# Top-k attention with two MLPs: decoding the first two 64-bit weights with one VectorE operation per two pieces

## The chip, the cores and the metric

One Trainium2 chip, one core of it. The metric is device time in microseconds (us) of one execution of the whole program. A core has five engines with instruction queues of their own, which run in order and wait for each other through semaphores: TensorE (PE in the profile), VectorE (DVE), ScalarE (ACT), GpSimd (POOL) and SyncE (SP), which here only issues transfers for the 16 DMA engines.

## What is computed

```python
def reference(q, k, v, moe_w_in, moe_w_out, moe2_w_in, moe2_w_out):
    scores = q @ k.T / sqrt(64)              # 4 batches, 8 heads, 576 x 576, head size 64
    keep the 32 largest of each row, softmax over them
    x = attn @ v                             # as 2304 tokens x 512
    h = x @ moe_w_in;  g = h * sigmoid(h);   x = g @ moe_w_out      # 512 -> 2048 -> 512
    h = x @ moe2_w_in; g = elu(h);           x = g @ moe2_w_out
    return x
```

q, k and v are float32. The four weights (512x2048 or 2048x512) arrive as float64: a weight is scaled by a 64-bit scalar when it is drawn. One weight is 8.4 MB.

## The kernel before

**Tiles and slots.** The 2304 tokens make 18 chunks of 128 rows, and with 8 heads 144 tiles. The program is one sequence of slots, `slot(s)`, from -4 on; the order of every engine's queue is written out there by hand. Slot s holds the scores of tile s+1 (TensorE, `emit_qk`), the first half of the top-k of tile s and the second half of that of tile s-1 (VectorE: four MAX8 and three MATCH_REPLACE8, then the mask, line 590), the exponential (ScalarE, line 582), the split of the exponentials into two float16 halves (ScalarE line 610, GpSimd line 616), their transpose by DMA (line 619) and the product with V of tile s-3 (`emit_av`). From slot 12 (`LAG`) on it also holds a step of the first MLP, from slot 24 on one of the second (`emit_in`, line 695, and `emit_out`, line 743). Slots 0 to 11 hold no MLP step.

**Weights.** Each weight is 16 pieces of 128x512 numbers, 512 KB in float64. `w_load` (line 240) brings a piece as 1024 32-bit words to a staging place; `w_rest` (259) replaces the low word of each number by its top bits as an integer, on ScalarE (line 263) or GpSimd (265); `w_dec_ops` (267) makes the float32 bit pattern of the high word by two VectorE operations, masking and shifting the lower 27 bits into a PSUM tile y (278), then putting sign and top exponent bit to it (281); GpSimd adds the remainder (284). `PIECES` (807) says how many pieces are decoded in slots -2, -1, 0 and so on: 3, 3, then 5 per slot, 3 in slot 11. Slots -2 to 1 decode weight 0, slots 2 to 5 weight 1, slots 5 to 8 weight 2, slots 8 to 11 weight 3. `dv` (965) places them: after each top-k operation up to `per` decode operations are issued. Ten pieces of weight 3 are staged and decoded in halves of 256 columns, in buffers of the MLP that are still unused (`rows`, line 212).

**Scales and splits.** When a weight is decoded, `w_gram` (291) sums its squares on TensorE, `w_trace` (301) reduces that on VectorE, and `w_ops` (306) makes a power of two as its scale. Then each piece is split into two float16 halves. At a point of a slot (`w_point`, 919: p = 0, 1 or 2) TensorE forms the low halves of two pieces (`w_lo`, 320, lines 322 and 323), ScalarE writes them (`w_put`, line 327) and makes the high halves of two later pieces (`w_hi`, line 316, one operation of 1024 elements). `free` (896) lists the points that may be used; slots 3 to 11 use 3, 3, 2, 0, 3, 3, 1, 3, 3 of them.

**Loads.** All transfers are issued by SP in the order of the slots: at a slot's start loads of Q, K and V, the transpose `et` of the exponentials, then the weight loads of `wload` (line 983); at its end transposes of Q and K (`q_tp`, `k_tp`, lines 515 and 411) and the weight loads of `wnow`. The pieces of weight 0 are issued from slot -4 on: 2, 4, 2, 3, 5 in slots -4 to 0; later ones a slot before their decode, as far as the staging place is free (`freed`, 218). The first K transposes belong to slot -2.

Of the kernel before, what the change touches and what calls it, by code (L numbers as in the profile page):

```python
# [32 lines left out]
def kernel(  # L33
# [172 lines left out]

    sW = {}
# [7 lines left out]
        [16, 18, 20, 22, 24, 26, 28, 30, 14, 12, 16, 18, 20, 22, 24, 26],  # L215
        ["tt", "gg", "ux", 30, 28, 26, 24, "tt", "gg", "ux", 30, 28, "tt", "gg", (WEND - 1, "6"), "ux"],
# [4 lines left out]
        [(1, n) for n in range(8)] + [(1, 15), (1, 14)] + [(2, n) for n in range(6)],  # L221
        [(1, 15)] * 3 + [(2, 7), (2, 6), (2, 15), (2, 14)] + [(3, n) for n in range(5)] + [(3, 7), (3, 8), (3, 10), (3, 9)],
# [35 lines left out]

    def w_rest(j, n, e=None):
        low = raws[j, n, e].rearrange("p (x two) -> p x two", two=2)[:, :, 0]  # L260
        top = raws[j, n, e].bitcast(U16).rearrange("p (x four) -> p x four", four=4)[:, :, 1]
        if slot_now[0] < ON_ACT or n % 2 == 0:
            nc.scalar.activation(out=low, in_=top, func=AF.Copy, scale=2.0 ** -13)
        else:
            nc.gpsimd.tensor_scalar(low, top, 2.0 ** -13, 0.0, op0=ALU.mult, op1=ALU.add)

    def w_dec_ops(j, n, e=None):
        f = w_raw(j, n, Wi)
        if e is not None:
            f = f[:, e * 256:(e + 1) * 256]  # L270
        def word(x):
            return raws[j, n, e].rearrange("p (x two) -> p x two", two=2)[:, :, x]

        y = []

        def first():
            y.append(ps_h.tile([128, 512], F32, tag="h0", name="y").bitcast(I32)[:, 0:f.shape[1]])
            nc.vector.tensor_scalar(y[0], word(1), 0x07FFFFFF, 3, op0=ALU.bitwise_and, op1=ALU.logical_shift_left)  # L278
# [669 lines left out]
    def slot(s):  # L948
# [170 lines left out]
```

## Time and profile before

| | |
|---|---|
| three runs | 1118.25, 1122.69, 1123.08 us; median 1122.69 us |
| profiled execution | 1125.6 us; its span from first to last instruction 1123.8 us |
| busy in the span | TensorE 997.1 us (89%), VectorE 954.2 (85%), ScalarE 877.8 (78%), GpSimd 816.2 (73%) |
| DMA | 141.34 MB moved |
| VectorE, two decode operations, slots 0 to 4 | 25 and 25 instructions, 34.2 us busy |

The page of the profile gives busy times of each engine, the span in 40 slices, the chain of work that ended last and groups of instructions by source line. The span is cut further below into windows that are the kernel's slots. A share over the whole span mixes the lead-in, in which the weights are decoded, with the long stretch of MLP steps; the views by window keep them apart.

### The profile page before, as it was taken

What the parts mean: (1) busy time and instruction counts of PE and PEld (TensorE: products, weight loads), DVE (VectorE), ACT (ScalarE), POOL (GpSimd) and SP (SyncE); (2) the same over time, 40 slices, a digit from 0 to 9 for tenths busy, and PEclk for the clock granted to TensorE, in tenths of its full rate; (3) what the DMA queues carried; (4) which work ended last, traced back from release to release, by engine and by line L of the source; (5) the groups of instructions that cost most, each with busy time, mean ns of one, the idle gap of its engine ahead of it and who ended that gap; (6) DMA issues with size and microseconds to landing.
All of it is one profiled execution on the core that took longest, in us unless ns stands there. A gap on an engine that the chain in (4) does not pass through costs nothing.

```text
span 1123.8 us, 30899 instructions
## 1 busy us (share of the span) xinstructions
PE 997.1 (89%) x11956; PEld 716.2 (64%) x11956; DVE 954.2 (85%) x2215; ACT 877.8 (78%) x1541; POOL 816.2 (73%) x1001
## 2 busy tenths in 40 slices
PE   0266679589989999999998999999999999999997
PEld 0223336367766777777766777777677777777755
DVE  5999998999887999999997999999899999994000
ACT  5577768989877898989887898988777777776554
POOL 5779886887767777777776777878767777776643
PEclk9978989889999999999999999999999999999999
DMA  9999883565577655566586757467864544433100
GB/s 307 302 256 259 255 206 84 92 98 115 111 136 127 120 102 113 117 115 132 108 149 133 138 103 126 103 119 135 135 115 87 100 82 82 82 68 58 29 20 10
DMA packets 385746, 141.34 MB, mean 126 GB/s; under 512 B 361536, under 2 KB 368704, under 8 KB 385600
## 3 DMA queue, kind: packets, MB, share of 16 engines
q1 hardware_dynamic: 385600, 139.38, 59.6%
q8 instruction: 93, 1.52, 0.6%
q14 instruction: 53, 0.43, 0.1%
HBM read 52.17 MB, written 21.10 MB: 65 GB/s over the span
## 4 chain that ended last, share of the span: by engine, by line
PE 39%; POOL 20%; issue 12%; DVE 11%; DMA 7%; ACT 6%; SPq 1%; POOLq 0%; ACTq 0%; DVEq 0%
PE h L695 17%; PE a L743 15%; POOL t L723 5%; POOL gh L162 4%; DVE m L567 3%; POOL e L616 3%; DVE r L571 3%; DMA xt<-x 3%; PE S L532 3%; PE av L635 2%; DVE y L278 2%; DMA et<-e 2%; POOL W L616 2%; POOL x L162 1%; DVE e L590 1%
## 5 line engine op out<-in xcount | busy, mean ns | idle before, releaser
L695 PE MATMUL h<-xt,W 128*128 128x128 f16 x6912 | 412.0, 220 | 8.6 <-DMA xt<-x 8.6
L695 PEld LDWEIGHTS <-W 128*128 128x128 f16 x6912 | 396.5, 98 | 22.1 <-DMA xt<-x 8.9
L743 PE MATMUL a<-W,gh 128*128 128x512 f16 x1728 | 399.0, 380 | 3.9 <-POOL gh L162 2.0
L567 DVE MAX8 m<-r 128x8 f32<-128x576 f32 x432 | 312.8, 749 | 2.6
L743 PEld LDWEIGHTS <-gh 128*128 128x128 f16 x1728 | 159.6, 98 | 178.8 <-POOL gh L162 4.8
L162 POOL TENSOR_TENSOR gh<-t,gh 128x512 f16<-128x512 f32 x144 | 167.3, 1162 | 73.7 <-ACT gh L727 73.7
L571 DVE MATCH_REPLACE8 r<-m,r 128x576 f32<-128x576 f32 x288 | 213.8, 742 | 0.0
L723 POOL TENSOR_TENSOR t<-u,t 128x512 f32<-128x512 f32 x144 | 183.4, 1273 | 29.8 <-ACT u L717 23.4
L582 ACT ACTIVATE e<-S,bias,c 128x576 f32<-128x576 f32 x144 | 119.8, 832 | 52.0 <-DVE r L571 36.4
L727 ACT ACTIVATE gh<-t 128x512 f16<-128x512 f32 x144 | 90.2, 627 | 88.5 <-POOL t L723 87.6
L616 POOL TENSOR_TENSOR e<-e,e 128x512 f16<-128x512 f32 x87 | 100.9, 1160 | 78.5 <-ACT e L610 74.2
L567 DVE MAX8 m<-S 128x8 f32<-128x576 f32 x144 | 109.6, 761 | 36.0 <-PE S L532 35.6
L532 PE MATMUL S<-kt,qt 128*128 128x288 f16 (+1 forms) x640 | 99.0, 295 | 36.1 <-DVE sv L134 18.7
L532 PEld LDWEIGHTS <-qt 128*128 128x128 f16 (+1 forms) x640 | 56.7, 102 | 110.2 <-issue 41.2
L590 DVE SCALAR_TENSOR_TENSOR e<-S,m,e 128x576 f32<-128x576 f32 x144 | 115.3, 801 | 0.1
L571 DVE MATCH_REPLACE8 r<-m,S 128x576 f32<-128x576 f32 x144 | 107.6, 747 | 0.0
L616 POOL TENSOR_TENSOR W<-e,W 128x512 f16<-128x512 f32 x57 | 66.2, 1161 | 44.0 <-ACT W L610 38.8
L635 PE MATMUL av<-vt,et 128*128 128x64 f16 (+1 forms) x2100 | 79.3, 194 | 12.9 <-DMA et<-e 12.9
L635 PEld LDWEIGHTS <-et 128*128 128x128 f16 (+1 forms) x2240 | 73.1, 101 | 21.3 <-DMA et<-e 14.8
L610 ACT ACTIVATE e<-e 128x576 f16<-128x576 f32 x87 | 58.9, 677 | 27.8 <-DVE e L590 15.1
L322 PE MATMUL lo<-W,eye 128*128 128x512 f32 x84 | 56.9, 766 | 20.1 <-ACT W L327 19.0
L284 POOL TENSOR_TENSOR W<-W 128x512 int32<-128x512 int32 (+1 forms) x55 | 68.9, 1282 | 7.5 <-DVE W L281 2.5
(126 smaller groups left out, 1265.3 us busy)
## 6 DMA issues: line engine op xcount, KB each, us to landing
W<-in_moe_w_in_dram SPq DMA_DIRECT2D x32, 512.0 KB, 7.1
W<-in_moe_w_out_dram SPq DMA_DIRECT2D x22, 512.0 KB, 5.1
qd<-q SPq DMA_DIRECT2D x34, 256.0 KB, 4.5
kn<-in_k_dram SPq DMA_DIRECT2D x16, 288.0 KB, 3.3
qn<-in_q_dram SPq DMA_DIRECT2D x16, 256.0 KB, 3.5
out_dram<-o SPq DMA_DIRECT2D x16, 256.0 KB, 2.4
vd<-v SPq DMA_DIRECT2D x12, 320.0 KB, 2.4
vt<-vd SPq DMA_DIRECT2D x22, 160.0 KB, 2.8
```

The lines of the kernel that those rows point to most:

```text
L162: nc.gpsimd.tensor_tensor(dst, x, hi, op=ALU.subtract)
L532: nc.tensor.matmul(out=ps[n * e:n * e + n, a, 0:HALF], lhsT=qt[:, 2 * (t % 2) + p, n * e:n * e + n], rhs=kT[bh][:, a * HALF:(a + 1) * HALF ...
L567: nc.vector.max(st["m8"][:, i, :], src if i == 0 else st["r"])
L571: nc.vector.match_replace(out=fold(r) if i == 0 else r, in_to_replace=st["m8"][:, i, :], in_values=src if i == 0 else r, imm_value=LOW,)
L582: nc.scalar.activation(out=fold(e), in_=src, func=AF.Exp, scale=c[:, 0:1], bias=bias)
L590: nc.vector.scalar_tensor_tensor(e, src, st["m8"][:, n - 1, 7:8], e, op0=ALU.is_ge, op1=ALU.mult, accum_out=sums[ch][:, j:j + 1])
L616: nc.gpsimd.tensor_tensor(h[:, S + LO:2 * S], e[:, 0:SF], h[:, 0:SF], op=ALU.subtract)
L635: nc.tensor.matmul(out=avs[ch][n * e:n * e + n, bh[1], :], lhsT=et[:, c, n * e:n * e + n], rhs=vT[bh][:, x, y:y + D], start=(i == 0), stop ...
L695: nc.tensor.matmul(out=ps[:, f:f + 128], lhsT=w, rhs=xt[:, z, :], start=(kk == 0 and x == 0), stop=(kk == KDM - 1 and x == 2),)
L723: nc.gpsimd.tensor_tensor(t, u, t, op=ALU.add if l else ALU.mult)
L727: nc.scalar.activation(out=gh[:, 0, :], in_=gf[l, ch, i], func=AF.Copy)
L743: nc.tensor.matmul(out=acc, lhsT=gh[:, z, u * 128:(u + 1) * 128], rhs=W[:, n, w * 512:(w + 1) * 512], start=(m == 0 and x == 0), stop=(m = ...
```

## The change

Weights 0 and 1 (`SIGNED`) get another decode, in pairs of pieces (1024 numbers). The high word is only shifted left by 3, in one VectorE operation for the pair; its second operand is a zero, one element in PSUM that is broadcast (`zero_at`). The shift loses the sign. ScalarE therefore writes the sign of each number as a bfloat16 plus or minus one into the upper half of the low word, after the remainder, and the addition on GpSimd adds sign, exponent offset and remainder together. The result is half the number, which `shift` of `w_ops` makes good. Remainders and additions of weights 0 to 2 and of the whole pieces of weight 3 are done in pairs; the two VectorE operations of those are as before, but the addition follows the last of them.

The work is laid out anew: `PIECES` is 2, 2, 6, 6, 4, 6, 6, 4, 6, 4, 5, 5, 5, 3, so weight 1 ends in slot 4. The loads of weight 0 are 3, 2, 0, 3, 8 in slots -4 to 0; weights 1 and 2 load 4, 6, 6, 4, 6, 4 in slots 1 to 6. Weight 3 has 12 pieces in halves, in another order of staging places, and more of its loads at the end of the slot ahead. The points (`POINTS`, with a fourth at a slot's end) are 1, 2, 1, 3, 4, 3, 1, 4, 2 in slots 3 to 11. In slot 0 decode operations follow only a top-k operation, and small operations left at a slot's end go ahead of left decode operations.

```diff
+    SIGNED = (0, 1)
+    PAIR = 2
...
-        [16, 18, 20, 22, 24, 26, 28, 30, 14, 12, 16, 18, 20, 22, 24, 26],
-        ["tt", "gg", "ux", 30, 28, 26, 24, "tt", "gg", "ux", 30, 28, "tt", "gg", (WEND - 1, "6"), "ux"],
+        [16, 18, 20, 22, 24, 26, 28, 30, 12, 14, 16, 18, 20, 22, 24, 26],
+        ["tt", "gg", 28, 30, "ux", "tt", "gg", "ux", "tt", "gg", 28, 30, "ux", "tt", (WEND - 1, "6"), "gg"],
...
+            if n % 2 == 0:
+                raws[j, n, e] = Wi[:, r:r + 2 * PAIR, :].rearrange("p a x -> p (a x)")
...
     def w_rest(j, n, e=None):
-        low = raws[j, n, e].rearrange("p (x two) -> p x two", two=2)[:, :, 0]
-        top = raws[j, n, e].bitcast(U16).rearrange("p (x four) -> p x four", four=4)[:, :, 1]
-        if slot_now[0] < ON_ACT or n % 2 == 0:
+        low = w_word(j, n, e, 0)
+        top = w_half(j, n, e, 1, U16)
+        if e is None and slot_now[0] < ON_ACT or e is None and n % 4 == 0 or e == 0:
             nc.scalar.activation(out=low, in_=top, func=AF.Copy, scale=2.0 ** -13)
         else:
             nc.gpsimd.tensor_scalar(low, top, 2.0 ** -13, 0.0, op0=ALU.mult, op1=ALU.add)
+        if j in SIGNED:
+            nc.scalar.activation(out=w_half(j, n, e, 1, BF16), in_=w_word(j, n, e, 1).bitcast(F32), func=AF.Sign)
 
     def w_dec_ops(j, n, e=None):
...
+        def rest():
             nc.vector.scalar_tensor_tensor(
-                f, word(1), -(1 << 30), y[0], op0=ALU.bitwise_and, op1=ALU.bitwise_or
+                f, w_word(j, n, e, 1), 3, zero_at().bitcast(I32).to_broadcast([128, m]),
+                op0=ALU.logical_shift_left, op1=ALU.bitwise_or
             )
-            nc.gpsimd.tensor_tensor(f, f, word(0), op=ALU.add)
-
-        return [first, second]
+            add()
+
+        def add():
+            nc.gpsimd.tensor_tensor(f, f, w_word(j, n, e, 0), op=ALU.add)
+
+        def halves(x):
...
+        if j in SIGNED:
+            return [rest]
+        return [o for x in range(0, m, 512) for o in halves(x)]
+
+    zero0 = ps_v.tile([128, H, D], F32, tag="av", name="zero")[:, 0, 0:1]
+    zero = {}
+
+    def zero_at():
+        s = slot_now[0]
+        if s < 3:
+            return zero0
+        if s not in zero:
+            zero[s] = Sps[s][:, 0, HALF + 64:HALF + 65]
+            nc.vector.memset(zero[s], 0.0)
+        return zero[s]
...
-        return pow2_ops(m, *sW[j])
+        return pow2_ops(m, *sW[j], 1 if j in SIGNED else 0)
...
-    PIECES = (3, 3, 5, 5, 5, 5, 5, 5, 5, 5, 5, 5, 5, 3)
+    PIECES = (2, 2, 6, 6, 4, 6, 6, 4, 6, 4, 5, 5, 5, 3)
     ON_ACT = 3
+    POINTS = {3: (2,), 4: (1, 2), 5: (2,), 7: (0, 1, 2, 3), 9: (2,), 10: (0, 1, 2, 3), 11: (0, 1, 2, 3)}
...
-            decs[s].append((j, *x))
+            if x[1] is not None or x[0] % 2 == 0:
+                decs[s].append((j, *x))
...
-    free = [(s, p) for s in range(ends[0] + 1, LAG + 1) for p in range(3) if p == 2 or s not in held]
+    free = [(s, p) for s in range(3, LAG) for p in POINTS.get(s, (0, 1, 2)) if p > 1 or s not in held]
...
-        wload[(-5, -5, -4, -4, -4, -4, -3, -3, -2, -2, -2, -1, -1, -1, -1, -1)[n]].append((0, n, None))
+        wload[(-5, -5, -5, -4, -4, -2, -2, -2, -1, -1, -1, -1, -1, -1, -1, -1)[n]].append((0, n, None))
...
                 if o:
                     o.pop(0)()
+                elif s == 0:
+                    continue
...
-        while small_ops or dec:
-            dv([])
+        while small_ops:
+            small_ops.pop(0)()
+            if s < 0 and dec:
+                dec.pop(0)()
+        while dec:
+            dec.pop(0)()
...
+        w_point(s, 3)()
...
+        nc.vector.memset(zero0, 0.0)
```

The function `halves` holds the two operations of before, unchanged, for each half of a pair.

## Rows read from the trace of the kernel before

**Rows 1.** Busy tenths of the span in 40 slices, from the page.

```profile
PE   0266679589989999999998999999999999999997
...
DVE  5999998999887999999997999999899999994000
```

**Rows 2.** Busy time in a window (length, engines, PEclk, DMA share, GB/s), body.

```profile
800.00:1000.00 200.00, 200.00 (x2598) 149.44 (x2597) 189.24 (x424) 155.40 (x274) 140.97 (x181) 1.00 0.51 92
```

**Rows 3.** The same view of slots 0 to 4 and slot 6.

```profile
20.57:31.09 10.52, 1.38 (x7) 0.60 (x5) 9.61 (x17) 8.16 (x17) 6.93 (x7) 1.00 1.00 368
31.09:43.92 12.83, 1.04 (x6) 0.72 (x7) 12.62 (x29) 4.09 (x7) 8.94 (x9) 1.00 1.13 333
43.92:56.78 12.86, 6.07 (x72) 5.43 (x70) 12.62 (x28) 8.73 (x19) 10.29 (x12) 0.86 0.85 259
56.78:69.61 12.83, 8.67 (x29) 3.65 (x28) 12.62 (x30) 6.50 (x10) 10.54 (x13) 0.63 1.05 276
69.61:82.12 12.51, 8.48 (x33) 3.54 (x32) 12.30 (x27) 12.18 (x24) 8.53 (x11) 0.84 0.96 245
...
95.59:109.51 13.92, 5.63 (x86) 4.89 (x84) 12.99 (x32) 7.83 (x16) 12.43 (x14) 0.81 1.03 279
```

**Rows 4.** Groups by line and shape, slots 0 to 4 (busy us, mean ns).

```profile
L284 POOL TENSOR_TENSOR W<-W 128x512 int32<-128x512 int32 x24 | 30.4, 1293 | 4.6 <-DVE W L281 2.3 <-issue 0.9 <-DMA vn<-in_v_dram 0.8
L281 DVE SCALAR_TENSOR_TENSOR W<-W,y 128x512 int32<-128x512 int32 x25 | 17.2, 687 | 0.9
L278 DVE TENSOR_SCALAR y<-W 128x512 int32<-128x512 int32 x25 | 17.0, 681 | 0.7 <-DMA W<-in_moe_w_in_dram 0.6
...
L316 ACT ACTIVATE W<-W,sw 128x1024 f16<-128x1024 f32 x5 | 5.7, 1150 | 0.3 <-DVE sw L134 0.3
...
L327 ACT ACTIVATE W<-lo 128x512 f16<-128x512 f32 x8 | 4.4, 589 | 0.2 <-PE lo L323 0.2
...
L263 ACT ACTIVATE W<-W 128x512 int32<-128x512 uint16 x20 | 12.0, 659 | 2.2 <-DMA W<-in_moe_w_in_dram 2.2
```

**Rows 5.** VectorE in order of time in slot 1 (start, length).

```profile
33.89 0.68 DVE L278 TENSOR_SCALAR y<-W 128x512 int32<-128x512 int32 x1
34.60 0.69 DVE L281 SCALAR_TENSOR_TENSOR W<-W,y 128x512 int32<-128x512 int32 x1
35.20 0.08 DVE L571 MATCH_VALUE_LOAD r<-m,r 128x8 f32 x1
```

**Rows 6.** Groups by shape at other sizes, in the lead-in.

```profile
L281 DVE SCALAR_TENSOR_TENSOR W<-gh,y 128x256 int32<-128x256 int32 x6 | 2.5, 421 | 0.3
...
L263 ACT ACTIVATE t<-t 128x256 int32<-128x256 uint16 x4 | 1.5, 429 | 0.0
...
L284 POOL TENSOR_TENSOR W<-W,t 128x256 int32<-128x256 int32 x6 | 4.3, 740 | 0.2 <-DVE p L131 0.2
...
L162 POOL TENSOR_TENSOR q<-qn,q 128x1024 f16<-128x1024 f32 x1 | 2.1, 2142 | 0.4 <-ACT q L484 0.4
```

**Rows 7.** Waits from 20 to 82 us (total us, times, longest).

```profile
ACT W L263 <- DMA W<-in_moe_w_in_dram: 2.2, 3, 1.2
```

**Rows 8.** Busy time in stretches of 2 us at the start.

```profile
10.00:12.00 2.00, 0.00 (x0) 0.00 (x0) 1.90 (x4) 1.25 (x3) 2.00 (x2) 1.00 1.02 411
...
16.00:18.00 2.00, 0.10 (x1) 0.00 (x0) 1.86 (x6) 1.54 (x3) 0.23 (x1) 1.00 1.45 93
```

**Rows 9.** The start in order of time, SP and VectorE.

```profile
12.99 3.72 SPq L411 DMA_TRANSPOSE kt<-k  x2
...
21.90 0.76 DVE L567 MAX8 m<-S 128x8 f32<-128x576 f32 x1
```

**Rows 10.** TensorE and VectorE in order of time, slots 12 and 13.

```profile
176.26 1.02 PE L322 MATMUL lo<-W,eye 128*128 128x512 f32 x2
...
189.32 0.16 DVE L131 TENSOR_SCALAR p<-gram 128x1 int32<-128x1 int32 x1 [1.28 <-PE gram L171]
```

**Rows 11.** The one table load, groups of ScalarE up to 180 us.

```profile
L156 ACT ACT_TABLE_LOAD x1 | 1.3, 1283 | 0.8 <-PEq L1103 0.8
```

More of the change, by code (lines that the diff above doesn't have):

```diff
@@ L220 @@
         [(0, n) for n in range(NWP)],
-        [(1, n) for n in range(8)] + [(1, 15), (1, 14)] + [(2, n) for n in range(6)],
-        [(1, 15)] * 3 + [(2, 7), (2, 6), (2, 15), (2, 14)] + [(3, n) for n in range(5)] + [(3, 7), (3, 8), (3, 10), (3, 9)],
+        [(1, n) for n in range(8)] + [(1, 14), (1, 15)] + [(2, n) for n in range(6)],
+        [(1, 15), (1, 15), (2, 6), (2, 7), (1, 15), (3, 0), (3, 1), (3, 4), (3, 5), (3, 6), (3, 2), (3, 3), (3, 7), (3, 8), (3, 11), (3, 9)],
     ]
@@ L265, in w_rest @@
             nc.gpsimd.tensor_scalar(low, top, 2.0 ** -13, 0.0, op0=ALU.mult, op1=ALU.add)
+        if j in SIGNED:
+            nc.scalar.activation(out=w_half(j, n, e, 1, BF16), in_=w_word(j, n, e, 1).bitcast(F32), func=AF.Sign)
     def w_dec_ops(j, n, e=None):
[L268 to L278, printed above, removed]
@@ L280, in second @@
-        def second():
+        x = j * NWP + n + OFF
+        if e is None:
+            f = Wi[:, x:x + PAIR, :].rearrange("p a x -> p (a x)")
+        else:
+            f = Wi[:, x, e * 256:(e + 1) * 256]
+        m = f.shape[1]
+        def rest():
             nc.vector.scalar_tensor_tensor(
-                f, word(1), -(1 << 30), y[0], op0=ALU.bitwise_and, op1=ALU.bitwise_or
-            )
-            nc.gpsimd.tensor_tensor(f, f, word(0), op=ALU.add)
-        return [first, second]
+                f, w_word(j, n, e, 1), 3, zero_at().bitcast(I32).to_broadcast([128, m]),
+                op0=ALU.logical_shift_left, op1=ALU.bitwise_or
+            )
+            add()
@@ new lines, in add, with first, second @@
+        def add():
+            nc.gpsimd.tensor_tensor(f, f, w_word(j, n, e, 0), op=ALU.add)
+        def halves(x):
+            y = []
+            z = slice(x, min(x + 512, m))
+            def first():
+                y.append(ps_h.tile([128, 512], F32, tag="h0", name="y").bitcast(I32)[:, 0:z.stop - x])
+                nc.vector.tensor_scalar(
+                    y[0], w_word(j, n, e, 1)[:, z], 0x07FFFFFF, 3, op0=ALU.bitwise_and, op1=ALU.logical_shift_left
+                )
+            def second():
+                nc.vector.scalar_tensor_tensor(
+                    f[:, z], w_word(j, n, e, 1)[:, z], -(1 << 30), y[0], op0=ALU.bitwise_and, op1=ALU.bitwise_or
+                )
+                if z.stop == m:
+                    add()
+            return [first, second]
@@ L876 @@
     per_slot = [s for s, c in zip(range(-2, 13), PIECES) for _ in range(c)]
-    dec = {j: {(n, None): per_slot[NWP * j + n] for n in range(NWP)} for j in range(4)}
+    dec = {j: {(n, None): per_slot[NWP * j + n] for n in range(NWP)} for j in range(3)}
+    dec[3] = {(n, None): s for n, s in zip((0, 1, 4, 2, 3, 5, 6, 7, 8, 9, 10, 11, 12, 13, 14, 15), per_slot[3 * NWP:])}
     dec[3] = {(n, e): s for (n, _), s in dec[3].items() for e in ((None,) if isinstance(rows[3][n], int) else (0, 1))}
```

6 lines of the change are left out of this document (5 added, 1 removed).

## The prediction, made before the change was run

> **What bounds the kernel now.** I read the page from the top: the busy tenths first, then the span cut into the kernel's own slots, then the groups inside the slots that the change touches. In the busy tenths [rows 1] VectorE stands at 9 in slices 2 to 6 (28 to 169 us) while TensorE stands at 2 to 7; TensorE is at 9 nearly all of the time from slice 10 on. In a long window far into the body TensorE is busy 200 us of 200 [rows 2]. So the run has two parts: a lead-in (slots -4 to 11), in which the weights are decoded, and a body in which TensorE is full. Work is issued slot by slot in a fixed order, so an earlier end of the lead-in is carried to the end one to one; a microsecond of VectorE in the body is worth nothing.
>
> I let a slot begin with VectorE's first operation in it, the third MAX8 of the tile before (in slot 0 its first decode operation): slot 0 at 20.57 us, slot 5 at 82.12. In slots 0 to 4 [rows 3] VectorE is busy 9.61, 12.62, 12.62, 12.62 and 12.30 us, 59.8 of 61.55. But the same rows warn: the packet time of the DMA engines adds up to 1.00, 1.13, 0.85, 1.05 and 0.96 of these slots, which weighted by their lengths is 61.4 of 61.55 us (it can pass 1, since packets of one engine overlap). ScalarE is busy 39.7 us there and GpSimd 45.2. VectorE is the bound by a narrow lead, and the transfers are next.
>
> **The decode of the first two weights (VectorE).** Today each piece costs two operations of 0.68 and 0.69 us [rows 4]. What they take on the engine is start to start: 0.71 from the first to the second and 0.60 to what follows, 1.31 together [rows 5]. The new single operation covers two pieces, 1024 elements. Its kind is that of the second operation, 421 ns at 256 elements [rows 6] and 687 at 512 [rows 4]: 266 ns per 256, so 687 + 2 x 266 = 1219 ns, less the same overlap of 0.09, is 1.13 us. Its second input is one zero, read over and over from PSUM; the old second operation read a full PSUM tile at the same place, so I see no reason for a dearer read (bounds: 1.13 and, if nothing overlaps, 1.22). Slots 0 to 4 decode 25 pieces today and 14 pairs afterwards: 25 x 1.31 - 14 x 1.13 = 32.8 - 15.8 = 17.0 us off VectorE. Each of slots 5 to 7 keeps the two-operation decode: 5, 5, 5 pieces become 4, 6, 4, that is -1.3 us in all. The zeroes are three one-element memsets at VectorE, costed at nothing beside 17 us. The changed exponent constant is the same operation.
>
> **What takes over in slots 0 to 4.** Three engines get their share worked out over the same five slots.
> - ScalarE: 20 remainders of 0.659 us leave (13.2), 11 remainders of pairs and 14 signs arrive. Price of each at 1024 elements: from 429 at 256 [rows 6] and 659 at 512 [rows 4], 230 per 256, it is 1.12 us; the 1024-element operation at line 316, 1.15 [rows 4], is the other bound. 25 x 1.12 = 28. Three of the six points (each two puts of 0.589 and one 1.15) move out of slots 3 and 4: -7.0. 39.7 - 13.2 + 28 - 7.0 = 47.5 us (durations taken out and put in; the overlaps of some 0.1 us are left aside on both sides).
> - GpSimd: 24 additions of 1.293 (31.0) become 14 of 1024 elements. From 740 at 256 [rows 6] and 1293 [rows 4]: 2.40 us; lower bound 2.14, the 1024-element subtraction [rows 6]. 45.2 - 31.0 + 33.6 = 47.8 us. Its remainders stay about as they were.
> - The transfers: the five slots moved 368 x 10.52 + 333 x 12.83 + 259 x 12.86 + 276 x 12.83 + 245 x 12.51 = 18.1 MB [rows 3], in which 25 pieces were issued. The changed slots issue 28, three of them put off from before slot 0, but the 4 of slot 4 aren't wanted before slot 5, so I keep the 18.1 MB. If all went at slot 0's 368 GB/s: 49.1 us. If the packet time can't be packed closer: 61.4 us. I take the rate of slots 0 and 1 together, the two that are full of loads: 8.14 MB in 23.35 us, 349 GB/s, so 51.9 us.
>
> VectorE would need 61.55 - 17.0 = 44.5 us. The largest of 44.5, 47.5, 47.8 and 51.9 decides: 51.9, a gain of 9.6 us rather than 17.0. VectorE, which hides the transfers today, then waits for pieces in flight: ScalarE already did three times, 1.2 us at the longest [rows 7]. Behind a VectorE operation that waits for a piece stand the next top-k operations of the slot; behind a ScalarE remainder that waits stand the tile's exponential and then its mask.
>
> The Trainium skill has a figure that speaks against this term: the page "DMA: Bandwidth & Descriptors", section "Where 436 GB/s comes from", gives about 358 GB/s as what one core gets from HBM, and says that this side binds. The rows don't bear it out as a ceiling, since a stretch of nothing but weight loads ran at 411 GB/s [rows 8]; by the page's figure the 18.1 MB would take 50.6 us, an estimate that would move the sum by 1.3 us.
>
> **The front (slots -4 to -1).** The first transposes of Q and K are issued behind 8 loads today, 5 afterwards; 3 x 512 KB at 411 GB/s [rows 8] is 3.8 us of queue. But SP reaches the K transposes only at 12.99 us and takes 3.72 for them [rows 9], and that does not move: the transposes of Q stand ahead of it. The first MAX8 is at 21.90 us, and its row names no idle time ahead of it: VectorE came from a decode operation. It may come up to 2.6 us earlier; on the other side the DMA engines, once the 5 loads are through, have little but transposes (93 GB/s in such a stretch [rows 8]), and what they don't load then is owed in slot 0, whose 8 loads come in one go ahead of the next transposes on SP's queue. I take 0, and -2.6 to +3.8 as the ends.
>
> **Slots 8 to 12.** The last weight is split in halves for 12 pieces instead of 10: a split piece takes four operations of 0.42 [rows 6] against two of 0.69, so +0.3 each, +0.6. Its buffers are reused sooner (more loads are issued only at the end of the slot ahead): 0 to 2.4 us, two waits of the longest kind of [rows 7]; I take 1.0. The moved points land in slots 6, 7 and 10: slot 6 had ScalarE busy 7.83 us of 13.92 [rows 3], and three points at 2.33 bring 14.8 in a slot that also gains one piece (1.3), so that just fits, and costs up to 1 us if it does not. One point less in slot 11 takes TensorE's last two pieces of lo out of slot 12's start (from 176.26 us on) and brings the trace of the last weight forward, for which VectorE waited 1.28 us [rows 10]: -1.0, between 0 and -1.3 on that row.
>
> **Sum.** -9.6 - 1.3 + 0.6 + 1.0 - 1.0 = -10.3 us. The profiled execution took 1125.6 us, of which the span is 1123.8; so 1115.3 for such an execution. It lies 2.9 us over the median of the runs shown, 1122.69, and the same step from there gives 1112.4: I forecast 1112.
>
> **Rivals.**
> - VectorE's saving comes through whole. For it: the loads sit in a queue a slot ahead, and a stretch of loads alone reached 411 GB/s [rows 8]. Against it: all of ScalarE, GpSimd and DMA would have to need under 45 us. With pieces in time the 1.0 for the reused buffers goes too: -17.0 - 2.6 (front) - 1.3 + 0.6 - 1.0 = -21.3: 1101 us.
> - The change only swaps the bound. For it: 61.4 us of packet time in 61.55, and ScalarE and GpSimd, both in order, each over 47 us with waits between them. Slots 0 to 4 stay near 60 us: -1.5 and the -0.7 of the sum's other terms, about -2: 1120 us.
> - Slower, by one mechanism: the DMA engines are the bound and are fed later. Place: slots -3 to 1. Price: 3.8 us of loading given away at the front and not won back, and 3.8 us more for the transposes of tiles 2 and 3, which then stand behind three more loads: +7.6 - 0.7 (the other terms of the sum), 1130 us. It decides once the packet time of slots 0 to 4 can't be pressed under 61 us; the 368 GB/s of slot 0 against 245 of slot 4 speak against it.
> - The sign needs another activation table than the exponential. One table load stands in the whole trace, 1283 ns [rows 11], with Square, Copy, Exp, Tanh, Relu and Identity in use, so a seventh function that needs one is unlikely: 0.03. If every one of the 14 signs in slots 0 to 4 were bracketed by loads, 28 x 1.28 = 36 us would join ScalarE's 47.5: 83 us, +22 in place of -9.6, about 1144 us. It turns slower from (61.55 - 47.5) / 1.28 = 11 loads on. The Trainium skill, page "ScalarE: Activation LUTs", section "Table sets: the hidden batching unit", says that cheap functions sit in every set as filler; it names relu, copy, identity and abs, not sign, and no row of this trace shows a sign.
>
> **How the numbers follow.** Forecast 0.48 (own range 1106 to 1117), whole saving 0.16, swapped bound 0.24, fed later 0.09, table 0.03. About 0.5% (5.6 us) is what a measurement of this kernel can tell from no change. Faster: 0.48 + 0.16 + 0.04 of the swapped bound = 0.68. Same: 0.20. Slower: 0.12. The range runs from 1101 (the whole saving) to 1121 (the swapped bound's middle and a little over): it leaves out half of the first, and both slower cases.
>
> **What would show it.** Right: slots 0 to 4 take 50 to 55 us, VectorE's share of them falls from 0.97 to about 0.83, with waits for W from DMA ahead of the new operation, 1.2 us long and 16 times; slots 8 to 11 as before; from slot 12 on the two runs are the same, shifted. Wrong: an operation far over 1.22 us; a second table load; VectorE still at 0.97 (the whole saving); or waits of VectorE on S (late transposes) in place of waits on W. The prediction fails most easily in the transfer term, since it stands on a mean rate.

## The result and the profile after the change

The change made the kernel slower: 1133.59 us median of 6 runs (1131.31 to 1136.88) beside 1122.88 of 6 runs of the kernel before (1118.25 to 1124.84); ratio 1.0102, 95% interval 1.0077 to 1.0127. The profiled execution took 1133.12 us, its span is 1131.4.

I cut the trace into the same slots as before, each from the third MAX8 of the tile ahead (slot 0 of the changed kernel from its first MAX8, at 17.78). All starts in us:

| kernel | slot 1 | slot 5 | slot 6 | slot 10 | slot 11 | slot 12 | slot 14 |
|---|---|---|---|---|---|---|---|
| before | 31.09 | 82.12 | 95.59 | 149.13 | 163.65 | 174.74 | 189.77 |
| after | 31.06 | 82.79 | 102.79 | 155.02 | 173.32 | 187.29 | 200.22 |

At slot 12 the changed kernel is 12.6 us late: +0.7 by slot 5, +6.5 in slot 5, -1.3 in slots 6 to 9, +3.8 in slot 10, +2.9 in slot 11. Slots 12 and 13 give 2.1 us back (12.9 us in place of 15.0), so slot 14 starts 10.5 us late, as much as the medians differ (10.7). From slot 14 to the end of the profiled execution it is 936 us before, 933 after, and between 931 and 937 in all the experiments below. So the whole question lies in the first 200 us.

The same stretches as [rows 3], of the changed kernel: slots 0 to 5, then 10 and 11 (length, busy time of PE, PEld, DVE, ACT, POOL with the operations, PEclk, DMA share, GB/s).

```profile
17.78:31.06 13.28, 1.47 (x6) 0.69 (x6) 6.57 (x10) 10.05 (x13) 6.21 (x4) 1.00 0.93 340
31.06:42.21 11.15, 1.04 (x6) 0.72 (x7) 9.76 (x22) 11.02 (x9) 7.39 (x4) 1.00 1.12 333
42.21:52.40 10.19, 5.88 (x72) 5.08 (x70) 8.61 (x20) 9.98 (x17) 7.95 (x7) 0.91 0.45 154
52.40:68.67 16.27, 2.12 (x22) 1.63 (x21) 9.92 (x25) 16.11 (x13) 12.33 (x11) 0.50 1.13 284
68.67:82.79 14.12, 8.73 (x32) 3.54 (x30) 9.59 (x21) 13.39 (x19) 10.96 (x11) 0.67 1.02 347
82.79:102.79 20.00, 10.76 (x92) 6.50 (x92) 11.19 (x30) 16.48 (x23) 13.18 (x10) 0.74 0.91 232
155.02:173.32 18.30, 13.09 (x39) 5.47 (x40) 14.01 (x34) 11.00 (x20) 14.81 (x22) 0.72 0.81 218
173.32:187.29 13.97, 10.57 (x39) 4.33 (x38) 10.30 (x25) 10.51 (x18) 8.89 (x14) 0.88 0.50 118
```

VectorE did get its work taken away: 44.5 us busy in slots 0 to 4 where [rows 3] add up to 59.8. But ScalarE is now full in slots 1 to 4: 11.02 of 11.15, 9.98 of 10.19, 16.11 of 16.27, 13.39 of 14.12. Which operation fills it is in the groups by line and shape, 8 to 95 us (busy us, mean ns), the answer to [rows 4]:

```profile
L277 ACT ACTIVATE W<-W 128x1024 bf16<-128x1024 f32 x16 | 39.6, 2504 | 1.0 <-POOL W L275 0.6
L295 POOL TENSOR_TENSOR W<-W 128x1024 int32<-128x1024 int32 x16 | 38.4, 2407 | 18.6 <-ACT W L277 14.5 <-ACT bias L625 4.2
L273 ACT ACTIVATE W<-W 128x1024 int32<-128x1024 uint16 x13 | 15.0, 1157 | 0.0
L288 DVE SCALAR_TENSOR_TENSOR W<-W,zero 128x1024 int32<-128x1024 int32 x10 | 12.2, 1219 | 11.2 <-DMA W<-in_moe_w_in_dram 9.7 <-DMA W<-in_moe_w_out_dram 1.5
...
L361 ACT ACTIVATE W<-W,sw 128x1024 f16<-128x1024 f32 x3 | 3.4, 1144 | 0.0
```

The decode operation (L288) takes 1219 ns, GpSimd's addition of a pair (L295) 2407, the remainder of a pair (L273) 1157: the prices of the forecast. The sign (L277), the same 1024 elements as L273 and L361, takes 2504 where 1120 was put down.

How that reaches VectorE: its waits in slots 0 to 5, and the order of events in slot 5 (ScalarE, TensorE, VectorE).

```profile
DVE W L288 <- DMA W<-in_moe_w_out_dram: 12.3, 8, 4.4
DVE gram L348 <- PE gram L343: 8.7, 1, 8.7
DVE W L288 <- DMA W<-in_moe_w_in_dram: 8.0, 5, 4.9
```
```profile
82.02 1.19 ACT L273 ACTIVATE W<-W 128x1024 int32<-128x1024 uint16 x1
83.24 4.79 ACT L277 ACTIVATE W<-W 128x1024 bf16<-128x1024 f32 x2
...
89.45 1.07 ACT L372 ACTIVATE W<-lo 128x512 f16<-128x512 f32 x2
...
90.08 2.08 PE L367 MATMUL lo<-W,eye 128*128 128x512 f32 x2 [7.53 <-ACT W L372]
...
95.40 3.83 PE L343 MATMUL gram<-W 128*128 128x128 bf16 x64 [0.69 <-ACT W L372]
...
99.35 0.30 DVE L348 SCALAR_TENSOR_TENSOR gram<-gram,eye 128x128 f32<-128x128 f32 x1 [8.74 <-PE gram L343]
```

Two signs in a row (83.24, 4.79 us) push back the exponential and the put of lo behind them; TensorE waits 7.53 us for that put and comes to weight 1's gram at 95.40, and VectorE stands 8.74 us for its trace. In slots 1 to 4 the same queue delays the transposes of the exponentials, and the loads stand behind these on SP's queue. In slot 2 the transpose goes out only at 50.06, 7.9 us after the slot's start, and the six loads at 51.47; that slot moved 154 GB/s at a DMA share of 0.45.

```profile
50.06 1.30 SPq L664 DMA_TRANSPOSE et<-e  x1
51.47 4.38 SPq L258 DMA_DIRECT2D W<-in_moe_w_out_dram  x6
```

Slots 10 and 11 have nothing to do with the sign: without it (`e2b_no_sign` below) they still take 17.48 and 13.78 us. Their long waits, VectorE and GpSimd in order of time:

```profile
164.08 1.11 POOL L275 TENSOR_SCALAR W<-W 128x1024 int32<-128x1024 uint16 x1 [2.80 <-DMA W<-in_moe_w_out_dram]
...
168.59 2.40 POOL L295 TENSOR_TENSOR W<-W 128x1024 int32<-128x1024 int32 x1
...
179.56 0.43 POOL L275 TENSOR_SCALAR x<-x 128x256 int32<-128x256 uint16 x1 [2.38 <-DMA x<-in_moe_w_out_dram]
```
```profile
171.02 0.42 DVE L308 SCALAR_TENSOR_TENSOR W<-u,y 128x256 int32<-128x256 int32 x1 [3.14 <-POOL W L295]
...
183.91 0.42 DVE L308 SCALAR_TENSOR_TENSOR W<-gh,y 128x256 int32<-128x256 int32 x1 [2.55 <-POOL W L295]
```

VectorE's half of piece 12 writes row 62, the staging place of pieces 10 and 11. Their pairwise addition (168.59 to 170.99) must be done first, and it stood behind a remainder that waited 2.80 us for its load. In slot 11 the first half of piece 15 writes row 65, where half of piece 14 is staged; that half's addition stood behind the remainder that waited 2.38 us. The two waits of VectorE, 3.14 and 2.55, are 5.7 of the 6.7 us that the two slots are longer.

### The profile page after: what moved, and what is told of

Its sections match the earlier page's. It is cut to its first block, busy times and chain, and to the rows that moved or that the text cites. A ratio compares the mean times of both kernels' runs of the same rounds, so it can differ in the third digit from the quotient of the medians.

```text
span 1131.4 us, 30829 instructions
## 1 busy us (share of the span) xinstructions
PE 996.7 (88%) x11956; PEld 716.3 (63%) x11956; DVE 931.6 (82%) x2174; ACT 912.2 (81%) x1539; POOL 813.2 (72%) x971
## 4 chain that ended last, share of the span: by engine, by line
POOL 26%; PE 26%; issue 13%; DVE 7%; ACT 6%; DMA 5%; POOLq 0%; SPq 0%; ACTq 0%; DVEq 0%
PE h L740 11%; PE a L788 11%; POOL t L768 7%; POOL gh L162 6%; POOL e L661 4%; POOL W L661 3%; DVE r L616 3%; DVE m L612 3%; DMA xt<-x 2%; PE S L577 2%; PE av L680 2%; POOL x L162 2%; ACT gh L772 1%; DMA et<-e 1%; POOL q L162 1%
## 5 line engine op out<-in xcount | busy, mean ns | idle before, releaser
L740 PEld LDWEIGHTS <-W 128*128 128x128 f16 x6912 | 397.6, 98 | 22.4 <-DMA xt<-x 10.5
L577 PEld LDWEIGHTS <-qt 128*128 128x128 f16 (+1 forms) x640 | 55.8, 101 | 108.4 <-issue 59.8
L295 POOL TENSOR_TENSOR W<-W 128x1024 int32<-128x1024 int32 (+1 forms) x27 | 63.1, 2343 | 27.6 <-ACT W L277 14.5
```

Source lines behind the costliest of these rows:

```text
L577: nc.tensor.matmul(out=ps[n * e:n * e + n, a, 0:HALF], lhsT=qt[:, 2 * (t % 2) + p, n * e:n * e + n], rhs=kT[bh][:, a * HALF:(a + 1) * HALF ...
L740: nc.tensor.matmul(out=ps[:, f:f + 128], lhsT=w, rhs=xt[:, z, :], start=(kk == 0 and x == 0), stop=(kk == KDM - 1 and x == 2),)
```

## The experiments

After a first round on the two suspects each was repaired, alone and together; then the remaining bound was tested. Where several runs were taken, a ratio to the kernel before is given, with its 95% interval.

**Why the sign takes 2.5 us: the function or the form of its write.**

```diff
 e1_copy
-  nc.scalar.activation(out=w_half(j, n, e, 1, BF16), in_=w_word(j, n, e, 1).bitcast(F32), func=AF.Sign)
+  nc.scalar.activation(out=w_half(j, n, e, 1, BF16), in_=w_word(j, n, e, 1).bitcast(F32), func=AF.Copy)
 e3_word
+  nc.scalar.activation(out=w_word(j, n, e, 0).bitcast(F32), in_=w_word(j, n, e, 1).bitcast(F32), func=AF.Sign)
```

> The 16 Sign operations of ScalarE (1024 float32 in, one bfloat16 of two bytes out in every eight) took 2.494 us each in the changed kernel, and the Copy of the remainder on the same engine, 1024 elements too, 1.154 us. Here the Sign becomes a Copy with the same operands; the sign of the weights is left out by that (a copied high half stands in its place), the work of all other engines stays. Theory FORM (the two-byte output with gaps makes it slow): the Copy takes 2.4 to 2.6 us too and the time stays at 1133, within 3. Theory FUNCTION (Sign itself is the slow one): the Copy takes 1.1 to 1.3 us, ScalarE is relieved of 16 x 1.3 = 21 us in slots 0 to 5 and the time falls to 1118 to 1125.

> The other half of the same question: the Sign stays but writes a whole float32 word (four bytes in every eight), over the remainder, which is left out of weights 0 and 1 by that. Theory FORM: the Sign now takes 1.1 to 1.3 us and the time falls to 1118 to 1125. Theory FUNCTION: it stays at 2.4 to 2.6 us and the time at 1133, within 3. If both this and the copy come out near 2.5, the stride or the float32 input is the cause.

The one line of each, groups by line and shape, first of the Copy, then of the Sign that writes a word:

```profile
L277 ACT ACTIVATE W<-W 128x1024 bf16<-128x1024 f32 x16 | 39.5, 2500 | 1.0 <-POOL W L275 0.6
```
```profile
L277 ACT ACTIVATE W<-W 128x1024 f32<-128x1024 f32 x16 | 18.1, 1136 | 1.6 <-POOL W L275 1.2
```

The form: a Copy into two bytes of every eight takes 2500 ns, a Sign into four bytes of every eight 1136. The input is the same in both, so neither the function nor the stride of the input costs anything. Two-byte results as such don't either: L361 above writes 1024 of them next to each other in 1144 ns. What is dear is two bytes with gaps; the width, the bfloat16 type and the place in the upper half of a word were not told apart. Times: 1131.94 and 1123.14 us, one run each.

**What the sign costs as a whole.**

```diff
 e2b_no_sign
-        if j in SIGNED:
-            nc.scalar.activation(out=w_half(j, n, e, 1, BF16), ..., func=AF.Sign)
-                f, w_word(j, n, e, 1), 3, zero_at()...
+                f, w_word(j, n, e, 1), 0, zero_at()...
```

> The 16 Sign operations are left out (the sign of weights 0 and 1 is lost; the shift of the decode is 0 bits in place of 3 so that the numbers stay finite, at the same size of operation). Theory SIGN (ScalarE, 16 x 2.5 = 40 us more in slots 0 to 5, is the whole of what went wrong up to slot 6): the start of slot 6 comes from 102.8 us back to before 88 us (before the change 95.6, less the 9.6 and 1.3 of the forecast, rounded), the 8.7 us wait for weight 1's gram in slot 5 is gone, and the time is 1133 - 15 = 1118 or less. Rival LOADS (the loads issued late, fewer ahead of the transposes, hold slots 0 to 4): VectorE still waits for DMAs 10 us or more over slots 0 to 4, slot 5 starts at 80 to 83 us as before the change, and only the wait for the gram comes back: 1125 to 1128. If the time stays over 1130, neither holds.

Measured 1122.20 us, ratio 0.9994 (0.9975 to 1.0014): 11.4 us better than the changed kernel, and level with the kernel before. Slot 5 starts at 77.68, slot 6 at 89.57, and the wait for the gram is 0.6 us. So theory SIGN holds for slot 5, and short of its number for slots 0 to 4. The rival holds in part: VectorE still waits 15.2 us for loads in slots 0 to 4, 5.8 of them in slot 4, but slot 5 starts earlier than the 80 to 83 it asked for.

**Slots 10 and 11.** `e4_w3` puts back for weight 3 alone the staging rows, what frees them, the order of the pieces, the single (unpaired) decode and the rule for the remainders.

> The changed kernel with weight 3 as it was before the change: its rows, the order and the single pieces of its decode, and what frees them; weights 0 to 2 as changed. Slot 10 was 3.8 us longer and slot 11 2.9 us longer than in the kernel before. Theory REUSE (the staging rows of weight 3, two pieces waiting for the same places and for GpSimd's pairwise adds): both slots come back to 13.7 and 14.6 us and the time is 1133.6 - 6.7 = 1127, between 1125 and 1129. Rival PASSED ON (the two slots are longer because the phase ahead of them runs late, or the gain is lost again behind slot 14): the time is 1131 to 1136.

Measured 1127.91 us, ratio 1.0042 (1.0025 to 1.0060): 5.7 us of the 6.7 came back. Slots 10 and 11 take 14.80 and 11.30, 6.2 us less than in the changed kernel, and slot 12 takes 0.6 more (the expectation named 13.7 and 14.6, which are about the lengths of slots 9 and 10 before the change; 14.52 and 11.09 are the right ones). `e11_rest` tells one part of it apart, in the kernel whose Sign writes a word:

```diff
-        if e is None and slot_now[0] < ON_ACT or e is None and n % 4 == 0 or e == 0:
+        if e is None and slot_now[0] < ON_ACT or n % (2 if j == 3 else 4) == 0:
```

> The kernel whose Sign writes a whole word (remainder of weights 0 and 1 left out), weight 3 as changed, except for one rule: which engine takes the remainders of weight 3. ScalarE takes all of an even piece and GpSimd all of an odd one, as before the change, in place of first halves to ScalarE and second halves to GpSimd. Slots 10 and 11 took 17.95 and 13.18 us there, 14.52 and 11.09 before the change. Theory RULE (in slot 11 GpSimd's pairwise add, for whose rows VectorE waited 2.55 us, stood behind its remainder of piece 14's second half): slot 11 falls to 11.0 to 11.8, slot 10 stays at 17 or more, 1123.1 - 1.7 = 1121. Rival PLACES (the staging places alone make both waits): both slots stay within 0.5.

Slots 10 and 11 of this kernel (columns as above):

```profile
142.16:160.72 18.56, 12.80 (x36) 5.33 (x37) 14.00 (x34) 12.09 (x21) 14.61 (x22) 0.63 0.92 230
160.72:172.16 11.44, 8.96 (x37) 3.72 (x36) 10.21 (x25) 10.32 (x18) 7.38 (x11) 1.00 0.42 101
```

Theory RULE for slot 11: 13.18 became 11.44. Slot 10 stays long, but with other waits: 2.5 us for a sum at TensorE, and GpSimd's at most 1.0. That the staging place of pieces 10 and 11 makes slot 10 long is read from the changed kernel's trace; which part of weight 3's new layout does it in every case stays open. The one run took 1117.26, but slot 5 already starts 2.3 us earlier than in the kernel it is compared with, so its time says little of slot 11.

**Both repairs together** (`e5_word_w3`: the Sign into a word, weight 3 as before).

> Both repairs at once: the Sign writes a whole word (1.14 us each in place of 2.49; the remainder of weights 0 and 1 is left out), and weight 3 as before the change. The first alone gave 1123.1, the second alone 1127.9 against 1133.6. Theory ADDS (two separate losses, one in slots 0 to 5, one in slots 10 and 11): 1133.6 - 10.5 - 5.7 = 1117.4, between 1116 and 1119. Rival PASSED ON (once slots 0 to 5 are short, slots 10 and 11 stand against something else, or the other way round): 1121 or more.

Measured 1117.34 us, ratio 0.9947 (0.9925 to 0.9969). Theory ADDS: the two losses are separate. The slots 1 to 5:

```profile
30.83:41.61 10.78, 1.05 (x6) 0.71 (x7) 9.76 (x22) 10.18 (x13) 10.02 (x6) 1.00 1.10 334
41.61:52.52 10.91, 6.42 (x74) 5.82 (x73) 8.62 (x21) 10.26 (x18) 8.89 (x9) 0.96 1.07 366
52.52:62.31 9.79, 1.90 (x22) 1.49 (x20) 9.71 (x24) 8.30 (x9) 9.62 (x9) 0.50 1.20 251
62.31:76.88 14.57, 7.58 (x31) 3.15 (x30) 9.58 (x20) 13.03 (x22) 11.16 (x11) 0.85 1.05 347
76.88:89.89 13.01, 11.01 (x95) 6.50 (x92) 11.20 (x30) 9.59 (x17) 9.91 (x9) 0.79 0.92 252
```

Slot 5 starts 5.2 us earlier than before the change, not 9.6. Slots 1 to 3 are two to three us shorter than [rows 3], slot 4 is two longer.

**The loads at the front** (`e7_front`: `wload` of weight 0 as before, on top of both repairs).

> As the kernel with both repairs, with weight 0's loads issued as before the change (8 ahead of the first transposes, 3 more before slot 0). Theory FED LATER (loading given away at the front is owed in slot 0): VectorE's wait of 6 us for weight 0 in slot 0 shrinks under 3, slot 1 starts 2 to 4 us earlier than at 31.9, and the time falls by as much. Rival EVEN (what the transposes lose, the loads win): the first MAX8 goes back to about 21.9 us, slot 1 starts at 31 to 32.5, and the time is within 1.5 of the kernel with both repairs.

Measured 1115.30 us, ratio 0.9938 (0.9920 to 0.9956); the interval overlaps that of the kernel without it. Theory FED LATER holds up to slot 1: it starts at 27.25 in place of 30.83, and the waits for weight 0 are 1.4 us in place of 6.6. But slot 5 starts at 76.71, only 0.2 earlier: slots 1, 3 and 4 grew by 0.6, 1.5 and 1.7 us, slot 4 to 16.24 with 6.6 us of waits for weight 1. Slot 5 is 1.2 shorter, and slot 14 starts 1.3 earlier.

**The order on the queue** (`e8_first`).

```diff
+    FIRST = (2, 3, 4)
...
+        if s in FIRST:
+            for x in wload[s - 1]:
+                w_load(*x)
         if 0 <= s - 2 < NTILE:
             emit_elo(s - 2)
```

> As the kernel with both repairs, but in slots 2, 3 and 4 the loads of weight 1 are put ahead of the transpose of the exponentials on the DMA queue (in slot 3 of the kernel without the Sign six of them were issued at 59.98, behind a transpose, 7.6 us after the slot's start, and VectorE waited 5.8 us for them in slot 4). Theory QUEUE (the loads are late because the transpose, which waits for ScalarE and GpSimd, is ahead of them): slot 4's waits for DMA fall under 3 us and the time by 2 to 4. Rival TRANSFERS (the DMA engines are full): the waits stay or move to the transposes, and the time is within 1, or higher.

Measured 1125.98 us, ratio 1.0030 (1.0014 to 1.0047), 8.6 more than without it. Rival TRANSFERS holds: slot 4's waits stay (5.1 us), slots 0 to 4 move 326 GB/s beside 332 without the new order, and the loads that now go first hold up the transposes. In slot 5 (22.73 us long) VectorE waits 6.1 us for TensorE, which itself had waited 6.5 us for a late transpose and 4.9 for ScalarE, and later 5.2 us for weight 1's gram, ahead of which TensorE waited another 3.2 us for ScalarE. The first of these waits:

```profile
DVE p L131 <- PE S L171: 6.1, 1, 6.1
```

**Are the transfers the next bound?** The 16 loads of weight 1 are left out, of the kernel with both repairs and the old front (`e9_noload`), and of the kernel before (`e10_before_noload`), one run each; the decode works on what lies there.

```diff
-        nc.sync.dma_start(out=t, in_=weights[j][r0:r0 + 128, c0:c0 + m])
+        if j != 1:
+            nc.sync.dma_start(out=t, in_=weights[j][r0:r0 + 128, c0:c0 + m])
```

> The kernel with both repairs and the old front loads, with the 16 loads of weight 1 (8.4 MB, wanted in slots 2 to 4) left out: its decode works on what lies in the staging rows. With the loads slots 0 to 4 ended at 76.7 us; slots 1, 2, 3 and 4 took 11.4, 10.6, 11.2 and 16.2, VectorE busy 9.8, 8.6, 9.8 and 9.6 in them, ScalarE 11.2, 10.4, 9.0 and 13.5. Theory TRANSFERS (the loads and their share of the DMA engines set the pace, as the forecast had it): slots 1 to 3 fall to 9 to 10 us each, slot 4 to 11 or less, slot 5 starts at 69 or before. Theory SCALARE (ScalarE's queue sets slots 1 to 3, and only slot 4's waits are for loads): slots 1 to 3 stay within 0.5 us each, slot 4 falls to 11 to 13, slot 5 starts at 71 to 74.

> The kernel before the change with the same 16 loads of weight 1 left out. Slots 1 to 4 took 12.83, 12.86, 12.83 and 12.51 us with VectorE busy 12.62, 12.62, 12.62 and 12.30. Theory of the forecast (VectorE is the bound there, the transfers lie beside it): the slots keep their lengths within 0.2 us each, and slot 5 starts at 81 to 82.2. Rival (the transfers, with a packet time of 61.4 of 61.55 us, hold it already): slot 5 starts at 79 or before.

Slots 1 to 5 of the first, and slots 2 and 3 of the second:

```profile
28.89:40.03 11.14, 1.04 (x6) 0.71 (x7) 9.76 (x22) 10.95 (x13) 10.70 (x7) 1.00 1.03 231
40.03:48.52 8.49, 7.09 (x86) 6.67 (x84) 8.42 (x21) 8.31 (x15) 7.07 (x8) 1.00 0.26 51
48.52:58.31 9.79, 1.13 (x8) 0.80 (x6) 9.71 (x24) 8.87 (x11) 9.62 (x9) 0.65 0.53 122
58.31:67.79 9.48, 6.45 (x24) 2.61 (x23) 9.40 (x21) 8.70 (x17) 9.39 (x9) 0.68 0.28 63
67.79:87.07 19.28, 12.43 (x101) 7.25 (x100) 11.40 (x29) 15.81 (x24) 15.06 (x12) 0.89 1.02 264
```
```profile
43.38:56.24 12.86, 6.38 (x72) 5.73 (x70) 12.62 (x28) 8.72 (x19) 10.28 (x12) 0.88 0.44 101
56.24:69.07 12.83, 9.00 (x29) 3.69 (x28) 12.62 (x30) 6.49 (x10) 10.56 (x13) 0.63 0.14 27
```

The kernel before keeps its slots to 0.02 us at DMA shares of 0.44 and 0.14: VectorE was its bound, as read. The repaired one, without weight 1's loads, runs slots 2 to 4 in 8.49, 9.79 and 9.48 us with VectorE full, and slot 5 starts at 67.79, 8.9 earlier: theory TRANSFERS for slots 2 to 4. But slot 12 starts only 0.7 us earlier than with the loads, slot 14 1.3, and the run took 1110.0. Slot 5 grows to 19.28 us, 7.0 of them a wait of VectorE for weight 1's gram: TensorE waits for the puts of lo on ScalarE again (4.9 us). Behind the transfers stands that chain.

**Without the remainder operations** that the Sign overwrites in these kernels (`e12_best`: they are taken out for weights 0 and 1).

> The kernel with both repairs and the old front loads, with the remainder operations of weights 0 and 1 taken out as well (there they were overwritten by the Sign; the remainder is left out of these weights as before): 16 operations of 1.14 us fewer, some 11 of them on ScalarE in slots 0 to 3, the rest on GpSimd in slots 3 and 4. Theory SCALARE (its queue sets slots 1 to 3): these fall from 11.4, 10.6 and 11.2 to 9.8 to 10.5 each, and the time from 1115.3 to 1111 to 1113. Theory TRANSFERS: the waits of VectorE for loads grow by what is saved, the slots stay within 0.5 each and the time within 1.5 of 1115.3.

Measured 1116.44 us, ratio 0.9945 (0.9928 to 0.9963): no gain in time, as theory TRANSFERS had it, but not in the way it said. Slots 1 to 3 took 11.05, 10.05 and 9.79, so slot 3 did fall (11.24 with the operations); slot 4 is 15.42, and VectorE waits 11.1 us for loads in slots 0 to 4, less than the 12.5 with the operations. Slot 5 starts 1.9 us earlier than with them, yet slots 5 and 9 are 0.5 and 0.9 longer, and at slot 14 only 0.3 is left.

**Keeping the remainder.** In the kernels above whose Sign writes a word it falls on the remainder. Two kernels kept it, as second input of VectorE's operation:

```diff
 e6_full
-                f, w_word(j, n, e, 1), 3, zero_at()...
+                f, w_word(j, n, e, 1), 3, w_word(j, n, e, 0),
...
+            nc.scalar.activation(out=w_word(j, n, e, 0).bitcast(F32), in_=w_word(j, n, e, 1).bitcast(F32), func=AF.Sign)
             add()
 e13_kept
+            nc.scalar.activation(out=w_out(j, n, e).bitcast(F32), in_=w_word(j, n, e, 1).bitcast(F32), func=AF.Sign)
...
-                f, w_word(j, n, e, 1), 3, zero_at()...
+                w_word(j, n, e, 0), w_word(j, n, e, 1), 3, w_word(j, n, e, 0),
```

> As the kernel with both repairs, but the remainder is kept: VectorE's operation takes it as its second input in place of the zero, and the Sign writes its whole word over it behind that operation. ScalarE has the same two operations for each pair, 1.15 and 1.14 us, at other places: the Sign now waits for VectorE. Theory SIZE (only the form of the write counts): within 2 of the kernel with both repairs. Rival ORDER (ScalarE, in order, is held by the Sign behind VectorE, and with it the exponentials): 3 to 6 us more than that kernel. VectorE's operation, with its second input from SBUF, 1.2 to 1.3 us.

> As the kernel with both repairs and the old front loads (1115.3), but the remainder of weights 0 and 1 is kept, so that nothing of the computation is left out: the Sign writes whole words into the rows of the decoded weight, VectorE's operation takes the remainder as its second input and writes over it, and GpSimd adds the two. ScalarE's Sign waits for nobody on VectorE. In the earlier kernel with the remainder VectorE's operation took 1.80 us and the time was 1131.0. Theory ORDER (that kernel lost by ScalarE's waits behind VectorE): VectorE gets 14 x 0.58 = 8 us more in slots 0 to 4, of which its idle time there (57 us long, 44 busy) hides most: 1115 to 1120. Theory TWO INPUTS (the 1.80 us operation, which GpSimd's additions run beside, is the loss): 1125 or more.

`e6_full` took 1130.96 us (1.0079, 1.0064 to 1.0094) with ScalarE waiting 14.1 us behind VectorE and the operation at 1800 ns on average; `e13_kept`, without that wait, 1134.45 (1.0093, 1.0062 to 1.0124), with the operation at 2272 ns. The first is far beyond what either of its theories named. In the second VectorE is busy 59.6 us in slots 0 to 4 beside 44.1 in `e7_front`, 15.5 of the 20.1 us by which these slots are longer; it also waits there for the remainder, on ScalarE and GpSimd, which it didn't need before. So theory TWO INPUTS holds in the main. VectorE and GpSimd of the second, in order of time (the operation once with GpSimd idle, and twice beside its additions):

```profile
16.09 1.23 DVE L296 SCALAR_TENSOR_TENSOR W<-W 128x1024 int32<-128x1024 int32 x1 [0.62 <-ACT W L275]
...
28.06 2.77 DVE L296 SCALAR_TENSOR_TENSOR W<-W 128x1024 int32<-128x1024 int32 x1
...
31.43 3.02 DVE L296 SCALAR_TENSOR_TENSOR W<-W 128x1024 int32<-128x1024 int32 x1
```
```profile
27.35 2.40 POOL L303 TENSOR_TENSOR W<-W 128x1024 int32<-128x1024 int32 x1
30.96 2.39 POOL L303 TENSOR_TENSOR W<-W 128x1024 int32<-128x1024 int32 x1 [1.22 <-DVE W L296]
```

## Why the prediction was wrong

**The step that failed first: the price of the sign.** The forecast put 14 signs at 1.12 us into ScalarE's 47.5 us and gave 1.15 as the other bound. Both prices came from rows that write whole words or neighbouring two-byte numbers [rows 4, 6]; no row of before writes two bytes with gaps, and the text took the number of elements for the whole price. At 2.50 us, 14 x 1.38 = 19.3 us are missing: 66.8, above the 51.9 of the transfers and above the 61.55 that the slots took. With that one number put right the forecast's own sum is +5.3 - 1.3 + 0.6 + 1.0 - 1.0 = +4.6, slower. It says so on the right side, and the +5.3 stands beside +7.2 at the start of slot 6, though not at its place: 0.7 came in slots 0 to 4, where ScalarE was busy 60.5 us with 12 of the signs, and 6.5 in slot 5, where the work that it had put off was wanted by the gram. With the sign in words ScalarE is busy 51.1 us in slots 0 to 4 (`e5_word_w3`), beside the 47.5 put down. But the sign alone does not make the forecast come true: at 1136 ns (`e3_word`) the time is 1123.14, no gain. The measured 1133.59 lies 21.2 us over the forecast of 1112.4; 10.5 of these go with the form of the sign's write (`e3_word`, one run), 5.7 with weight 3 (`e4_w3`), and the 4.9 that `e5_word_w3` keeps are, by subtraction, mostly the transfers'. The forecast had looked only for a wrong table for this operation. The Trainium skill, page "ScalarE: Activation LUTs", section "What ACT_TABLE_LOAD costs", has every function run at one element a cycle, for float32 and bfloat16 alike. That the function doesn't matter agrees with Copy and Sign here (2500 and 2504 ns with the same write); that the type doesn't matter fails for the write with gaps, 2500 ns in bfloat16 beside 1136 in float32.

**Weight 3's buffers: the mechanism was named, the size was off.** 1.0 us was put down for reused buffers, with two waits of 1.2 as the upper end [rows 7], and 0.6 for the split pieces. It cost 6.7 us in slots 10 and 11, and 5.7 came back when weight 3 was put back. The waits used as bound were for a load alone. Here a load that was late held GpSimd's queue, with the addition that frees VectorE's destination behind it: a wait of 2.80 us, and after it four additions of halves and the one of 2.40, became a wait of 3.14 at VectorE.

**The transfers in slots 0 to 4: right as the next bound, too small as a price.** `e9_noload` shows that they hold slots 2 to 4 once ScalarE is out of the way. 51.9 us came from 18.1 MB at the mean rate of two full slots, as the forecast itself feared. With both repairs the five slots took 59.22 us (columns as above):

```profile
17.66:76.88 59.22, 18.42 (x129) 11.87 (x130) 44.24 (x92) 51.09 (x71) 46.16 (x36) 0.87 1.06 332
```

Both factors were off: the rate is 332 GB/s in place of 349, and 332 x 59.22 is 19.7 MB in place of 18.1. The three pieces put off from the front, 1.6 MB, are loaded in these slots too; the forecast saw them and kept the 18.1. Slot 0 begins 2.9 us earlier than before and takes part of this up, so slot 5 starts 5.2 us earlier, not 9.6. Slot 3 moved only 251 GB/s, and slot 4 waits 4.9 us for loads. The order on the queue is not the reason: the DMA share of slot 3 is 1.20, the highest of the five, and with the loads put first the wait stayed (`e8_first`). The packets of slots 2 and 3 with both repairs show what fills it:

```profile
DMA packets 2194, 3.99 MB, mean 366 GB/s; under 512 B 1294, under 2 KB 1294, under 8 KB 2192
DMA packets 4761, 2.45 MB, mean 251 GB/s; under 512 B 4227, under 2 KB 4483, under 8 KB 4760
```

Small packets come with the transposes, the only transfers issued in slot 2 of `e9_noload`, where 1770 of 1771 packets are under 512 B. Slot 3 has over three times as many of them as slot 2, and moves fewer bytes in a fuller share. A mean rate of slots full of loads doesn't price such a slot.

**What held.** VectorE's saving: 44.5 us busy in slots 0 to 4, as put down, at 1.22 us for an operation. GpSimd's 2.40. VectorE as the bound of the kernel before (`e10_before_noload`). No second table load: the changed trace has one. Slots 5 to 7, with both repairs, take 38.0 us in place of 40.0 (-1.3 was put down). The end of the lead-in gave more than its 1.0: slots 12 and 13 are 2.1 us shorter. The wait for the last trace, 1.28 us [rows 10], is 0.91 after, and two waits of VectorE for the scores are gone, which the forecast had not counted (the kernel before, slots 12 and 13):

```profile
176.46 0.77 DVE L567 MAX8 m<-S 128x8 f32<-128x576 f32 x1 [0.96 <-PE S L532]
...
182.53 0.77 DVE L567 MAX8 m<-S 128x8 f32<-128x576 f32 x1 [0.27 <-PE S L532]
```

The front at nothing held in the number alone: slot 1 starts at 31.06 and 31.09, since the first MAX8 came 4.1 us earlier and VectorE then waited 6.7 us for weight 0. With the old front loads slot 1 of the repaired kernel starts at 27.25 in place of 30.83 (`e7_front`).

**The rivals.** "Slower, fed later" had the right side for a reason that did not decide: the old front loads win 3.6 us at slot 1, and slots 1 to 4 take 3.4 of them back. "Swapped bound" was the nearest to what happened, since ScalarE took VectorE's place, but its price stopped at no gain. The whole saving, 1101, did not come even without the loads of weight 1 (`e9_noload`, 1110.0): the gram in slot 5 is next.

**A faster kernel.** With the sign in a word, weight 3 as before and the old front loads, 1115.30 us beats both, with a ratio of 0.9938; it leaves out the remainder of weights 0 and 1. Neither of the two kernels that kept it with a word-wide sign was faster than before.

## What to carry to other kernels

Price an added operation by a row of the same form, not only of the same size: a narrow write with gaps more than doubled the cost of an operation whose engine and element count were known. Where work is moved from the bound to an engine with room, add up that engine's queue with the upper bound of each unknown price, and ask what else waits in that queue: here the late puts of lo cost 6.5 us in slot 5, where no decode was late. When a place in memory is reused sooner, the price is the whole chain that frees it, late load, in-order engine and addition, not one wait for one load.

## What the hardware showed that I had not expected

- ScalarE writing two bytes in every eight: 2500 ns for 1024 elements with Copy, 2504 with Sign. Four bytes in every eight: 1136. Two bytes next to each other: 1144. What makes the narrow write slow was not measured.
- VectorE's operation with both inputs in SBUF takes 1.23 us at 16.09, where GpSimd has nothing from 15.43 to 17.45, but 2.77 and 3.02 where GpSimd's addition runs at its start. In both of these cases it ends 1.08 to 1.10 us after the addition does (30.83 after 29.75, 34.45 after 33.35), nearly its whole time alone, so it gets next to nothing done until then. In the changed kernel, with its second input one zero in PSUM, it took 1.22 beside additions of the same size. The Trainium skill, page "SBUF — State Buffer", section "Who interferes with whom", says that a VectorE instruction with two SBUF inputs contends with a GpSimd instruction that reads SBUF, and that one with a single SBUF input does not (outside its two-port modes); these rows agree.
